# An attention and MoE kernel on one core: ScalarE's copy in the decoding of float64 weights moves 16 bits where it moved 8, and the due times of the order are new

## The chip, the core and the metric

One core of a Trainium2 chip (trn2) runs the whole program. TensorE (PE in the profile) multiplies, ScalarE (ACT), VectorE (DVE) and GpSimd (POOL) do everything else, and SyncE (SP) only issues DMAs. The metric is the device time of one execution in microseconds, the median of several runs.

## The reference

Eight batches of twelve heads of attention over 448 positions with head dimension 64, then a two-layer network with the gate h·cos(h):

```python
def _attn_ref(q, k, v, g_q, g_k):
    q_n, k_n = (rmsnorm(q, g_q), rmsnorm(k, g_k))          # over the last axis
    scores = 1/np.sqrt(64) * np.matmul(q_n, k_n.transpose(0, 1, 3, 2))
    attn = softmax(scores)
    return np.matmul(attn, v).astype(np.float32)           # (8, 12, 448, 64)

def _moe_ref(x, w_in, w_out):                              # x (3584, 768)
    h = x @ w_in                                           # w_in (768, 2048)
    g = h * np.cos(h)
    return (g @ w_out).astype(np.float32)                  # w_out (2048, 768)
```

The two weight matrices come as float64. The kernel reads them as pairs of 32-bit words and makes float32 of them on the chip.

## The kernel before, in words

**Units and phases.** Two heads make a unit `u`; there are 48 units, `NP` = 6 of them to a batch. The first six units are "plain" (float32 matmuls, `score_plain`, `pt_copy`, `av_plain`); all later ones split each operand into a high and a low part (`score`, `pt_high`, `pt_low`, `av`). For each unit PE makes seven score tiles S, DVE scales each by the row's norm and takes its row minimum (`rowmin`, L571), ACT takes the exponential into P (`expo`, L579), PE transposes P into the banks PT0 and PT1 (L613, L618), ACT and DVE copy those to SBUF (L636 and L670 on ACT; L643, L645 and L668 on DVE), and PE multiplies by v (L660, L678). The results of six units are a batch's x; ACT copies them into `xs` (`x_split`, L726) after POOL has scaled them by the row sums (`x_norm`, L717), and then the first layer `ffn1` (L744 to L746) can run on them, 16 blocks of weights `wi` to a batch. The attention of the next batch and `ffn1` of the last one share PE. After the attention comes the second layer (L818 to L820), with PE alone setting the pace.

**The decoding.** Each of 16 blocks of w_in is loaded as 128 x 1536 int32 (`w_load`, `raw` in the profile), and decoded in four steps (`decode`, called by `w_decode`): step 0 on ACT scales the upper words into float32 (L263); step 1 on ACT moves bits of the lower word to the bottom of the upper word (L266); step 2 on DVE shifts the upper word down and keeps its sign and its three lowest bits (L268); step 3 on DVE shifts step 0's result up by three and ORs these bits in (L270). Then ACT rounds the block to its high part (`w_high`, L280) and DVE subtracts that from it (`w_low`, L285). The w_out blocks take the same `decode` with half the width, 32 times (`v_decode`, `rawo` in the profile), between 190 and 861 us.

**What sets the order.** Each engine runs its instructions in the order in which they are written. The class `Plan` writes that order: every piece of work has an engine, a cost, a due time and the keys it reads and writes; a list scheduler takes, on each engine, the ready piece that is due first. The tables `SHIFT`, `PAIR` and `BEGIN` move the due times by kind of work and by unit. `order` uses the costs and due times only while it builds the program; on the chip only the order remains, with semaphores for the dependencies. An instruction whose input is late holds up all that stands behind it on its engine.

Of the kernel before, what the change touches and what calls it, by code (L numbers as in the profile page):

```python
# [13 lines left out]
U8 = mybir.dt.uint8  # L14
# [11 lines left out]
class Plan:  # L26
# [123 lines left out]
    YIELD, AHEAD, WITHIN, UNTIL = ("x_norm", "w_low"), "k_norm", 4.0, 60.0  # L150
# [20 lines left out]
def tile_attention_moe(  # L171
# [14 lines left out]
    NP = NU // B  # L186
    NQT = 7
# [158 lines left out]
    kboth, qlow = {}, [apool.tile([128, 768], F32R, tag="E0", name="E0", bufs=1)]  # L346
# [18 lines left out]
    def e_clear(i):  # L365
        if i:
            qlow.append(apool.tile([128, 768], F32R, tag="E1", name="E1", bufs=1))
# [85 lines left out]
    def rkb(u):  # L453
        return (qtwo[u % 2][:, :S] if u < NP else kboth[u % 2][:, S:]).bitcast(F32)

# [3 lines left out]
    def rk_load(u):  # L459
        if u < NP + 2:  # L460
# [10 lines left out]
    def k_norm(u):  # L471
        if u >= NP:
# [17 lines left out]
    def q_scale(u):  # L490
        q = q_plain(u) if u < NP else qd
        nc.gpsimd.tensor_scalar(q, q, gsc[u < NP], 0.0, op0=ALU.mult, op1=ALU.add)

# [35 lines left out]
    def place(u, n):  # L529
        i = 7 * min(u, NP) + (n if u < NP else 0)  # L530
        if u < NP:
            return ("ph", i // 4) if i % 4 == 3 else ("S", 3 * (i // 4) + i % 4)
        return ("S", i - i // 4 + 7 * (u - NP) + n)

    NSP = 7 * NP // 4
# [72 lines left out]
    def transp(u, kc, part, last):  # L608
        k = KS[kc]
        if kc < 3:  # L610
            for i, t in enumerate(TILES[part]):
                c = k + 64 * (t > 3)
                nc.tensor.transpose(pt[part][:, i * 128 : i * 128 + 128], p_rows(u, t)[:, c : c + 128], ident)  # L613
        else:
            flat = pbuf.rearrange("p n s -> p (n s)")
            for t in range(3):
                e = S * (p_slot(p_key(u, t)) + 1)
                nc.tensor.transpose(pt[0][:, t * 128 : t * 128 + 128], flat[:, e - 64 : e + 64], ident)  # L618
            c, n = (k - 64, 128) if u < NP else (k, 64)
# [215 lines left out]
    def y_store(b, oc, src):  # L835
# [5 lines left out]
        "av": (5.3, 39.33, 0.0), "av3": (-13.83, 15.47, 0.0), "av_plain": (0.0, 0.0, 10.94),  # L841
        "d_place": (7.71, -0.4, 0.0), "e_clear": (2.06, 0.0, 0.0), "e_place": (-13.2, 0.0, 0.0),
        "expo": (7.95, 14.26, -11.58), "ffn1": (-3.18, -2.89, 0.0), "g_fold": (0.0, 0.0, 3.13),
        "g_load": (0.0, 0.0, 0.98), "h_both": (-29.07, 0.0, 0.0), "h_out": (-14.91, 5.31, 0.0),
        "h_store": (-0.09, 0.0, 0.0), "k_high": (7.68, 8.19, 0.0), "k_load": (0.0, 0.0, 1.22),
        "k_low": (33.26, 1.74, 0.0), "k_norm": (45.02, 0.0, -0.54), "kn_copy": (0.0, 0.0, -13.33),
        "kn_load": (0.0, 0.0, -45.16), "kn_norm": (0.0, 0.0, -20.32), "kn_pow": (0.0, 0.0, 29.13),
        "kn_reduce": (0.0, 0.0, -2.77), "kn_square": (0.0, 0.0, -6.31), "kn_turn": (0.0, 0.0, 1.63),
        "kq_load": (-17.42, -14.74, 0.0), "m_place": (-18.39, 4.08, 0.0), "pt_copy0": (0.0, 0.0, -3.9),
        "pt_copy1": (0.0, 0.0, -44.97), "pt_high0": (-25.09, -5.18, 0.0), "pt_high1": (-9.32, -33.28, 0.0),  # L850
        "pt_low0": (-20.85, 10.99, 0.0), "pt_low1": (-5.79, -41.16, 0.0), "q_high": (-79.7, 2.11, 0.0),
        "q_load": (0.0, 0.0, 5.21), "q_low": (-2.0, 3.7, 0.0), "q_scale": (-57.44, -11.45, -3.1),
# [12 lines left out]
    }
    PAIR = (18.33, 10.11, -12.21, 0.63, 7.01, 13.7, -4.94, -21.21, -1.78, 0.0, -39.42, -0.16)
    BEGIN = {"v_load": -5.46, "q_load": 4.31, "v_fetch": -9.59, "st_load": -5.63, "w_load": 12.81, "k_load": 10.48, "kq_load": -37.77, "v_plain": -2.91}

    def add(eng, cost, due, fn, *args, **more):
# [3 lines left out]
        if name in ("ffn1", "h_out", "h_store", "h_both", "x_split"):  # L873
            stage = int(first < (NP if name == "x_split" else 1))
        elif name[:2] not in ("w_", "v_", "e_") or name in ("v_load", "v_high", "v_low", "v_plain", "e_place"):
            stage = 2 if first < NP else int(first < NP + 3)
# [5 lines left out]
        if name in ("w_load", "w_decode", "w_high", "w_low"):  # L882
            due += -0.33 * first
        if name in ("ffn1", "h_out", "h_store", "h_both") and not first:
            due += -0.23 * args[1]
        if name in ("v_fetch", "v_decode", "v_sum", "v_split", "v_store"):
            due += 2.55 + 25.482 * first
# [3 lines left out]
        if more.get("start"):  # L891
            late = BEGIN.get(name0, 0.0) + (0.075 * first if name0 == "w_load" else 0.0)
            more["start"] = max(0.0, more["start"] + late)
# [9 lines left out]
    def base(u):  # L903
        return 14.0 + (PER0 * u if u < NP else PER0 * NP + PER * (u - NP))
# [7 lines left out]
    def weights(fc):  # L912
# [4 lines left out]
        if f64:  # L917
            for step, eng, cost in ((0, ACT, 0.84), (1, ACT, 0.84), (2, DVE, 0.74), (3, DVE, 1.27)):
# [3 lines left out]
        for hf in range(2):  # L922
            add(DVE, 0.53, d, w_low, fc, hf, nc.vector, r=[f, w], w=[("wlo", fc, hf)])
# [40 lines left out]
    def prepare(u):  # L964
# [4 lines left out]
        turned, plain = u < NKT, u < NP  # L969
# [21 lines left out]
        add(SP, ISS, D0 - 45, st_load, u, w=sd, kb=224.0 if turned else 448.0, start=0.0 if u < NP else D0 - 60)  # L991
# [32 lines left out]
    def attend(u):  # L1024
        D0 = base(u)
        b, cc = divmod(u, NP)
        plain = u < NP
        step = 3.0 if plain else 4.0
        lead = 0.0 if u < NP else None
# [127 lines left out]
    for b in range(B):  # L1157
# [5 lines left out]
        if not b:  # L1163
            for i in range(RING["E"]):
                add(DVE, 0.56, 24.0 + 45 * i, e_clear, i, w=[("E0", i)] + [("km", 4)] * i + [("E", NP + i)], start=20.0)
# [188 lines left out]
```

## Time and profile before

| | |
|---|---|
| median of three runs | 1362.52 us (1362.02 to 1363.71) |
| profiled execution | 1365.0 us, of which the program's span is 1363.2 us |
| PE busy | 1339.7 us, 98% of the span, 6998 matmuls |
| DVE busy | 1013.0 us, 74% |
| ACT busy | 977.6 us, 72% |
| POOL busy | 579.1 us, 42% |
| copies of 8 bits on ACT, w_in | 16, 31.7 us in all |
| copies of 8 bits on ACT, w_out | 32, 34.6 us in all |

The span runs from the first instruction to the last one. The busy shares are means over stages that differ: the stretch up to 125 us, where the plain units run and most of w_in is decoded, the stretch up to about 250 us, and the rest.

### The profile page before, as it was taken

To read this page: it belongs to the slowest core of one execution; us is meant where nothing else is said; L and a number is where in the kernel's file an instruction comes from. 1 tells how busy PE (TensorE), PEld (TensorE's weight loads), DVE (VectorE), ACT (ScalarE), POOL (GpSimd) and SP (SyncE) were. 2 spreads that over 40 slices of the span, in tenths; PEclk is the share of its full clock that TensorE was granted. 3 is DMA by queue.
4 is the path that set the end of the run, shared out by engine and by line. 5 is a ranking of instruction groups with operands and counts; after the bars stand their busy time and mean duration, and the time that the engine had idled before them with its cause. 6 is when DMAs were issued, how large, how long until landed. Compare 5 with 4: busy or idle time off the path is not lost.

```text
span 1363.2 us, 21477 instructions
## 1 busy us (share of the span) xinstructions
PE 1339.7 (98%) x6998; PEld 1173.4 (86%) x6998; DVE 1013.0 (74%) x1795; ACT 977.6 (72%) x1920; POOL 579.1 (42%) x522
## 2 busy tenths in 40 slices
PE   6998999999999999999999999999999999999998
PEld 3447888988989899899898889999999999999998
DVE  5988887677777767677767776518889889889743
ACT  7999988787887888787887787646566366366321
POOL 4576657676765866765765675310000000000000
PEclk9998999999999999999999999999999999999999
DMA  6998879889898898898888878248989369369334
GB/s 209 263 286 221 178 192 236 227 240 245 237 234 219 216 245 222 212 256 227 215 221 229 219 208 225 88 176 278 332 287 311 111 246 315 107 246 316 104 113 153
DMA packets 149472, 302.19 MB, mean 222 GB/s; under 512 B 34368, under 2 KB 83088, under 8 KB 149360
## 3 DMA queue, kind: packets, MB, share of 16 engines
q1 hardware_dynamic: 149360, 300.83, 76.8%
q8 instruction: 55, 0.90, 0.3%
q14 instruction: 57, 0.47, 0.1%
HBM read 193.99 MB, written 62.73 MB: 188 GB/s over the span
## 4 chain that ended last, share of the span: by engine, by line
PE 87%; ACT 5%; DVE 3%; POOL 2%; issue 2%; DMA 1%; SPq 0%; ACTq 0%; POOLq 0%; DVEq 0%
PE y L819 10%; PE y L818 10%; PE y L820 10%; PE ph L744 9%; PE ph L745 9%; PE ph L746 9%; PE S L567 8%; PE PT L613 7%; PE O L660 5%; PE O L662 3%; ACT P L579 1%; PE y L746 1%; PE y L744 1%; PE y L745 1%; PE PT L618 1%
## 5 line engine op out<-in xcount | busy, mean ns | idle before, releaser
L571 DVE TENSOR_SCALAR_CACHE_REDUCE S<-S,r 128x448 f32<-128x448 f32 x336 | 224.8, 686 | 59.4 <-PE S L567 49.6
L744 PE MATMUL ph<-xs,wi 128*128 128x448 f32 x660 | 250.7, 380 | 0.2 <-ACT hbuf L762 0.2
L819 PE MATMUL y<-g,wo 128*128 128x448 f32 x672 | 245.4, 365 | 0.0
L818 PE MATMUL y<-g,wo 128*128 128x448 f32 x672 | 245.4, 365 | 0.0
L820 PE MATMUL y<-g,wo 128*128 128x448 f32 x672 | 245.4, 365 | 0.0
L745 PE MATMUL ph<-xs,wi 128*128 128x448 f32 x660 | 242.2, 367 | 0.0
L746 PE MATMUL ph<-xs,wi 128*128 128x448 f32 x660 | 241.4, 366 | 0.0
L579 ACT ACTIVATE P<-S,sm 128x448 f32<-128x448 f32 x336 | 214.4, 644 | 26.2 <-DVE S L571 23.7
L800 ACT CAST g<-gq 128x896 fp32r<-128x896 f32 x112 | 105.7, 943 | 172.8 <-PE y L820 172.3
L636 ACT CAST hi<-PT 128x512 fp32r<-128x512 f32 (+1 forms) x336 | 172.5, 538 | 73.1 <-PE PT L620 42.9
L643 DVE TENSOR_TENSOR lo<-PT,hi 128x512 fp32r<-128x512 f32 x252 | 151.4, 617 | 49.3 <-ACT hi L636 48.7
L798 DVE TENSOR_TENSOR g<-gq,g 128x896 fp32r<-128x896 f32 x112 | 122.0, 1089 | 61.5 <-ACT g L800 61.1
L613 PEld LDWEIGHTS PT<-ident,P 128*128 128x128 f32 x1008 | 120.7, 140 | 37.0 <-ACT hi L670 6.0
L613 PE MATMUL PT<-ident,P 128*128 128x128 f32 x1008 | 146.2, 274 | 1.8 <-DVE lo L643 1.5
L744 PEld LDWEIGHTS ph<-xs,wi 128*128 128x128 f32 x660 | 124.4, 188 | 13.9 <-ACT hbuf L762 1.4
L819 PEld LDWEIGHTS y<-g,wo 128*128 128x128 f32 x672 | 126.2, 188 | 10.0
L820 PEld LDWEIGHTS y<-g,wo 128*128 128x128 f32 x672 | 126.2, 188 | 10.0
L818 PEld LDWEIGHTS y<-g,wo 128*128 128x128 f32 x672 | 126.2, 188 | 10.0
L746 PEld LDWEIGHTS ph<-xs,wi 128*128 128x128 f32 x660 | 124.2, 188 | 10.7
L745 PEld LDWEIGHTS ph<-xs,wi 128*128 128x128 f32 x660 | 124.7, 189 | 8.7
L399 POOL TENSOR_TENSOR r<-r,nhalf 128x14 f32<-128x14 f32 (+1 forms) x48 | 122.6, 2554 | 4.0
L660 PE MATMUL O<-hi,vs 128*128 128x448 f32 x336 | 118.7, 370 | 0.0
(125 smaller groups left out, 2588.4 us busy)
## 6 DMA issues: line engine op xcount, KB each, us to landing
wo<-wo_d SPq DMA_DIRECT2D x152, 384.0 KB
gq<-h_d SPq DMA_DIRECT2D x64, 448.0 KB
h_d<-hbuf SPq DMA_DIRECT2D x54, 448.0 KB
wo_d<-ao SPq DMA_DIRECT2D x56, 384.0 KB
sd<-sd SPq DMA_DIRECT2D x46, 448.0 KB
kq<-kq SPq DMA_DIRECT2D x42, 480.0 KB
D<-qhi SPq DMA_DIRECT2D x84, 192.0 KB
raw<-w_in SPq DMA_DIRECT2D x16, 768.0 KB
```

The lines of the kernel that those rows point to most:

```text
L571: nc.vector.tensor_scalar(d["S", t][:, :S], d["S", t][:, :S], d["r"][:, t : t + 1], None, op0=ALU.mult, op1=ALU.min, accum_out=d["sm"][:, ...
L579: nc.scalar.activation(p_rows(u, t), d.pop(("S", t))[:, :S], AF.Exp, bias=sm[:, 1, t : t + 1], scale=-1.0, accum_out=sm[:, 2, t : t + 1],)
L613: nc.tensor.transpose(pt[part][:, i * 128 : i * 128 + 128], p_rows(u, t)[:, c : c + 128], ident)
L636: nc.scalar.copy(hi if kc < 3 else hi[:64], pt_rows(u, kc, part))
L643: nc.vector.tensor_tensor(lo, src, hi.bitcast(F32), ALU.subtract)
L660: nc.tensor.matmul(O, st, d["hi", kc][:, HEADS[hh]], start=(kc == 0), stop=(kc == 3))
L744: nc.tensor.matmul(ph[:, :S], whi, x2[:, 0, :], start=(cc == 0), stop=False)
L745: nc.tensor.matmul(ph[:, :S], whi, x2[:, 1, :], start=False, stop=False)
L746: nc.tensor.matmul(ph[:, :S], wlo, x2[:, 0, :], start=False, stop=(cc == NCC - 1))
L818: nc.tensor.matmul(y, whi, hi[:, e], start=first and e == 0, stop=False, **more)
L819: nc.tensor.matmul(y, whi, lo[:, e], start=False, stop=False, **more)
L820: nc.tensor.matmul(y, wlo, hi[:, e], start=False, stop=last and e == NG - 1, **more)
```

## The change

In step 1 of `decode` ACT copies, in every 8-byte pair of words, 16-bit number 1 (the upper half of the lower word) over 16-bit number 2 (the lower half of the upper word); before, it copied byte 3 over byte 4. Step 2 then shifts by 13 in place of 5, so that the same three bits arrive in the same place. The number of elements of each of the four steps stays as it was. In the planner, the costs of step 3 on DVE (1.27 to 1.0) and of `w_low` (0.53 to 0.6) are other numbers, that of step 1 stays 0.84, and all the due times are new. `w_low` leaves the list `YIELD`. `NF` = 6 takes the place of `NP` where "plain" is meant (both are 6), and the tile `E0` is made in `e_clear`.

```diff
-            by = st.bitcast(U8).rearrange("p (n t) -> p n t", t=8)
-            nc.scalar.copy(by[:, :, 4], by[:, :, 3])
+            words = st.bitcast(U16).rearrange("p (n t) -> p n t", t=4)
+            nc.scalar.copy(words[:, :, 2], words[:, :, 1])
         elif step == 2:
-            nc.vector.tensor_scalar(up, up, 5, SIGN_LOW, op0=ALU.arith_shift_right, op1=ALU.bitwise_and)
+            nc.vector.tensor_scalar(up, up, 13, SIGN_LOW, op0=ALU.arith_shift_right, op1=ALU.bitwise_and)
...
-    YIELD, AHEAD, WITHIN, UNTIL = ("x_norm", "w_low"), "k_norm", 4.0, 60.0
+    YIELD, AHEAD, WITHIN, UNTIL = ("x_norm",), "k_norm", 4.0, 60.0
...
-        "w_load": (-3.56, 0.0, 0.0), "w_low": (2.76, 0.0, 0.0), "x_half": (-1.22, 1.78, 0.0),
+        "w_low": (8.87, 0.0, 0.0), "x_half": (-15.11, 3.84, 0.0), "x_norm": (-0.93, -13.53, 2.55),
...
-            for step, eng, cost in ((0, ACT, 0.84), (1, ACT, 0.84), (2, DVE, 0.74), (3, DVE, 1.27)):
+            for step, eng, cost in ((0, ACT, 0.84), (1, ACT, 0.84), (2, DVE, 0.74), (3, DVE, 1.0)):
...
-            add(DVE, 0.53, d, w_low, fc, hf, nc.vector, r=[f, w], w=[("wlo", fc, hf)])
+            add(DVE, 0.6, d, w_low, fc, hf, nc.vector, r=[f, w], w=[("wlo", fc, hf)])
```

What the new due times do to the order is small in most places. All engines keep their counts of instructions but for a few; what moves is some places up or down. Lines of the changed kernel are one higher than those of the kernel before (L266 is L267 there). The first number in a name is the unit or the block: `hi5_0` is the copy of unit 5's transposed P, `S7_0` a score tile of unit 7, `raw8` block 8 of w_in, counted from 0.

The first place is on ACT, near 86 us of the profile before, where the plain units end. Before:

```order
L266 COPY raw7_577<-raw7_577 128x768
L579 ACTIVATE P_109,sm5_707<-S5_2_785,sm5_707 128x448
L726 CAST xs_837<-xf0_324 128x448
L726 CAST xs_837<-xf2_596 128x448
L670 COPY hi4_2_847<-PT0_110 128x512
L579 ACTIVATE P_109,sm5_707<-S5_3_812,sm5_707 128x448
L579 ACTIVATE P_109,sm6_827<-S6_3_828,sm6_827 128x448
L495 CAST qhi7_862<-kq_108 128x512
L670 COPY hi5_0_870<-PT0_110 128x512
```

And of the change:

```order
L580 ACTIVATE P_108,sm5_728<-S5_2_786,sm5_728 128x448
L671 COPY hi4_2_838<-PT0_109 128x512
L727 CAST xs_841<-xf0_324 128x448
L727 CAST xs_841<-xf2_613 128x448
L727 CAST xs_841<-xf3_720 128x448
L727 CAST xs_841<-xf1_508 128x448
L580 ACTIVATE P_108,sm5_728<-S5_3_829,sm5_728 128x448
L496 CAST qhi7_864<-kq_107 128x512
L703 COPY xf4_869<-O4_0_761 64x448
L588 ACTIVATE sm5_728<-sm5_728 128x7
L671 COPY hi5_0_881<-PT0_109 128x512
```

`hi4_2` now stands ahead of the copies into `xs`, and the copy of block 7 has gone further up; four copies into `xs` now stand together ahead of `hi5_0`.

The second place is on DVE, from 108 to 117 us of the profile before (`lo6_1` and `lo6_2` free the banks into which PE transposes next). Before:

```order
L268 TENSOR_SCALAR raw8_631<-raw8_631 128x768
L643 TENSOR_TENSOR lo6_1_1055<-PT0_110,hi6_1_1048 128x512
L643 TENSOR_TENSOR lo6_1_1055<-PT1_111,hi6_1_1048 128x384
L592 COPY rt6_1069<-PT1_111 7x128
L270 SCALAR_TENSOR_TENSOR wf8_1003<-wf8_1003,raw8_631 128x768
L571 TENSOR_SCALAR S7_0_1071,sm7_988<-S7_0_1071,r7_681 128x448
L571 TENSOR_SCALAR S7_4_1076,sm7_988<-S7_4_1076,r7_681 128x448
L571 TENSOR_SCALAR S7_5_1082,sm7_988<-S7_5_1082,r7_681 128x448
L285 TENSOR_TENSOR wi8_1102<-wf8_1003,wi8_1102 128x384 x2
L268 TENSOR_SCALAR raw9_673<-raw9_673 128x768
L643 TENSOR_TENSOR lo6_2_1130<-PT0_110,hi6_2_1126 128x512
```

And of the change, from the same `lo6_1` on (the step on block 8 has moved up to stand just ahead of `lo6_0`, and step 3 of that block ahead of these rows):

```order
L644 TENSOR_TENSOR lo6_1_1057<-PT0_109,hi6_1_1046 128x512
L572 TENSOR_SCALAR S7_0_1052,sm7_990<-S7_0_1052,r7_691 128x448
L644 TENSOR_TENSOR lo6_1_1057<-PT1_110,hi6_1_1046 128x384
L593 COPY rt6_1082<-PT1_110 7x128
L572 TENSOR_SCALAR S7_4_1059,sm7_990<-S7_4_1059,r7_691 128x448
L572 TENSOR_SCALAR S7_5_1064,sm7_990<-S7_5_1064,r7_691 128x448
L286 TENSOR_TENSOR wi8_1070<-wf8_960,wi8_1070 128x384 x2
L572 TENSOR_SCALAR S7_1_1103,sm7_990<-S7_1_1103,r7_691 128x448
L394 TENSOR_REDUCE r10_1130<-sd10_1012 128x14
L644 TENSOR_TENSOR lo6_2_1136<-PT0_109,hi6_2_1125 128x512
```

Step 2 of block 9 has gone from just ahead of `lo6_2` to behind it, and one row minimum and one sum of squares have come in its place.

The third place is the start of SP's queue (`kn` are the first unit's keys, `gs` the gains). Before:

```order
L413 DMA kq_108<-kn 112x512
L413 DMA kn1_116<-kn 112x512
L386 DMA sd0_118<-sd 128x448 x2
L228 DMA gs_93<-gg 128x4
L488 DMA q6_99<-kq 128x512 x2
```

And of the change:

```order
L229 DMA gs_93<-gg 128x4
L414 DMA kq_107<-kn 112x512
L387 DMA sd0_116<-sd 128x448
L414 DMA kn1_118<-kn 112x512
L387 DMA sd0_116<-sd 128x448
L489 DMA q6_99<-kq 128x512 x2
```

The load of the gains is now issued first, ahead of the first keys.

## Rows read from the trace of the kernel before

**Rows 1.** Busy us (instructions) of PE, PEld, DVE, ACT, POOL by stretch; clock, DMA share, GB/s.

```profile
20.00:95.00 75.00, 71.66 (x322) 32.01 (x323) 64.80 (x145) 70.37 (x140) 42.95 (x37) 1.00 0.91 275
95.00:125.00 30.00, 26.19 (x122) 18.33 (x121) 26.12 (x52) 27.17 (x58) 23.59 (x21) 0.89 1.07 259
125.00:250.00 125.00, 122.04 (x673) 108.13 (x672) 105.89 (x219) 113.71 (x239) 82.25 (x70) 1.00 0.81 194
250.00:1350.00 1100.00, 1099.61 (x5814) 1001.58 (x5813) 804.68 (x1355) 754.92 (x1459) 419.47 (x380) 1.00 0.76 223
110.00:120.00 10.00, 6.19 (x28) 4.77 (x28) 10.00 (x18) 9.56 (x20) 6.35 (x7) 0.79 1.08 255
120.00:130.00 10.00, 10.00 (x52) 9.04 (x51) 7.87 (x16) 8.06 (x17) 6.49 (x6) 0.87 0.80 174
```

**Rows 2.** Groups of instructions, whole span: busy us, mean ns of one, idle before them.

```profile
L571 DVE TENSOR_SCALAR_CACHE_REDUCE S<-S,r 128x448 f32<-128x448 f32 x336 | 224.8, 686 | 59.4 <-PE S L567 49.6 <-PE S L551 3.5 <-POOL r L398 2.4
L393 DVE TENSOR_REDUCE r<-sd 128x14 f32<-128x896 f32 (+1 forms) x48 | 50.9, 1061 | 4.1 <-ACT sd L390 3.9
L266 ACT COPY rawo<-rawo 128x384 uint8<-128x384 uint8 x32 | 34.6, 1082 | 0.6
L266 ACT COPY raw<-raw 128x768 uint8<-128x768 uint8 x16 | 31.7, 1982 | 0.1
L263 ACT ACTIVATE aq<-rawo 128x384 f32<-128x384 f32 x32 | 17.9, 560 | 1.3 <-POOL ao L328 1.1
L263 ACT ACTIVATE aq<-raw 128x768 f32<-128x768 f32 x8 | 7.6, 947 | 1.2 <-issue 1.2
```

**Rows 3.** Timeline near 69 us: start, us, engine, line; in brackets idle time before, and what ended it.

```profile
67.06 1.96 ACT L266 COPY raw<-raw 128x768 uint8<-128x768 uint8 x1
68.70 0.68 ACT L579 ACTIVATE P<-S,sm 128x448 f32<-128x448 f32 x1
69.52 0.64 PE L551 MATMUL S<-km,q 128*128 128x448 f32 x1 [1.13 <-ACT P L579]
```

**Rows 4.** Timeline near 88 us.

```profile
86.02 2.01 ACT L266 COPY raw<-raw 128x768 uint8<-128x768 uint8 x1
...
88.27 1.13 ACT L726 CAST xs<-xf 128x448 fp32r<-128x448 f32 x2
...
89.20 0.69 ACT L670 COPY hi<-PT 128x512 f32<-128x512 f32 x1
...
89.94 0.59 PE L678 MATMUL O<-hi,vs 128*64 128x448 f32 x1 [0.99 <-ACT hi L670]
```

**Rows 5.** Timeline from 107 to 117 us.

```profile
107.75 0.88 DVE L268 TENSOR_SCALAR raw<-raw 128x768 int32<-128x768 int32 x1 [1.45 <-ACT raw L266]
...
109.37 1.99 ACT L266 COPY raw<-raw 128x768 uint8<-128x768 uint8 x1
...
112.87 0.63 ACT L579 ACTIVATE P<-S,sm 128x448 f32<-128x448 f32 x1
...
113.65 0.47 PE L567 MATMUL S<-M,D 128*128 128x448 f32 x1 [1.08 <-ACT P L579]
...
114.90 1.49 DVE L268 TENSOR_SCALAR raw<-raw 128x768 int32<-128x768 int32 x1
...
116.31 1.14 DVE L643 TENSOR_TENSOR lo<-PT,hi 128x512 fp32r<-128x512 f32 x2
...
117.04 0.69 PE L618 MATMUL PT<-ident,P 128*128 128x128 f32 x2 [2.72 <-DVE lo L643]
```

**Rows 6.** Timeline near 222 us, the copy of a w_out block.

```profile
219.79 1.09 ACT L266 COPY rawo<-rawo 128x384 uint8<-128x384 uint8 x1
...
224.75 0.47 PE L567 MATMUL S<-M,D 128*128 128x448 f32 x1 [1.11 <-ACT P L579]
```

**Rows 7.** Timeline of SP's queue at the start; the second number is the issue.

```profile
2.58 0.43 SPq L228 DMA_DIRECT2D gs<-gg  x1
```

**Rows 8.** Timeline of POOL near 72 us.

```profile
72.41 0.70 POOL L492 TENSOR_SCALAR kq<-kq,gs 128x512 f32<-128x512 f32 x1 [4.99 <-DMA kq<-kq]
```

More of the change, by code (lines that the diff above doesn't have):

```diff
@@ L13 @@
 I32 = mybir.dt.int32
-U8 = mybir.dt.uint8
+U16 = mybir.dt.uint16
 AF = mybir.ActivationFunctionType
@@ L186, in tile_attention_moe @@
     NP = NU // B
+    NF = 6
     NQT = 7
@@ L453, in rkb @@
     def rkb(u):
-        return (qtwo[u % 2][:, :S] if u < NP else kboth[u % 2][:, S:]).bitcast(F32)
+        return (qtwo[u % 2][:, :S] if u < NF else kboth[u % 2][:, S:]).bitcast(F32)
     def rk_spread(u):
@@ L490, in q_scale @@
     def q_scale(u):
-        q = q_plain(u) if u < NP else qd
-        nc.gpsimd.tensor_scalar(q, q, gsc[u < NP], 0.0, op0=ALU.mult, op1=ALU.add)
+        q = q_plain(u) if u < NF else qd
+        nc.gpsimd.tensor_scalar(q, q, gsc[u < NF], 0.0, op0=ALU.mult, op1=ALU.add)
     def q_high(u):
@@ L529, in place @@
     def place(u, n):
-        i = 7 * min(u, NP) + (n if u < NP else 0)
-        if u < NP:
+        i = 7 * min(u, NF) + (n if u < NF else 0)
+        if u < NF:
             return ("ph", i // 4) if i % 4 == 3 else ("S", 3 * (i // 4) + i % 4)
-        return ("S", i - i // 4 + 7 * (u - NP) + n)
-    NSP = 7 * NP // 4
+        return ("S", i - i // 4 + 7 * (u - NF) + n)
+    NSP = 7 * NF // 4
     def score_plain(u, j):
@@ L618, in transp @@
                 nc.tensor.transpose(pt[0][:, t * 128 : t * 128 + 128], flat[:, e - 64 : e + 64], ident)
-            c, n = (k - 64, 128) if u < NP else (k, 64)
+            c, n = (k - 64, 128) if u < NF else (k, 64)
             nc.tensor.transpose(pt[0][:n, 384:512], p_rows(u, 3)[:, c : c + n], ident)
@@ L875, in add @@
         elif name[:2] not in ("w_", "v_", "e_") or name in ("v_load", "v_high", "v_low", "v_plain", "e_place"):
-            stage = 2 if first < NP else int(first < NP + 3)
+            stage = 2 if first < NF else int(first < NF + 3)
         if name in ("pt_low", "pt_high", "pt_copy", "transp"):
@@ L882, in add @@
         if name in ("w_load", "w_decode", "w_high", "w_low"):
-            due += -0.33 * first
+            due += 0.109 * first
         if name in ("ffn1", "h_out", "h_store", "h_both") and not first:
-            due += -0.23 * args[1]
+            due += -0.497 * args[1]
         if name in ("v_fetch", "v_decode", "v_sum", "v_split", "v_store"):
-            due += 2.55 + 25.482 * first
+            due += -1.02 + 25.026 * first
         other = ("w_load", "w_decode", "w_high", "w_low", "v_fetch", "v_decode", "v_sum", "v_split", "v_store", "e_clear")
@@ L891, in add @@
         if more.get("start"):
-            late = BEGIN.get(name0, 0.0) + (0.075 * first if name0 == "w_load" else 0.0)
+            late = BEGIN.get(name0, 0.0) + (0.042 * first if name0 == "w_load" else 0.0)
             more["start"] = max(0.0, more["start"] + late)
@@ L903, in base @@
     def base(u):
-        return 14.0 + (PER0 * u if u < NP else PER0 * NP + PER * (u - NP))
+        return 14.0 + (PER0 * u if u < NF else PER0 * NF + PER * (u - NF))
     def ffn_due(b, i):
@@ L990, in prepare @@
             add(SP, ISS, D0 - 34, kq_load, u, w=kd + qd, kb=480.0, start=D0 - 40)
-        add(SP, ISS, D0 - 45, st_load, u, w=sd, kb=224.0 if turned else 448.0, start=0.0 if u < NP else D0 - 60)
+        add(SP, ISS, D0 - 45, st_load, u, w=sd, kb=224.0 if turned else 448.0, start=0.0 if u < NF else D0 - 60)
         if plain:
@@ L1026, in attend @@
         b, cc = divmod(u, NP)
-        plain = u < NP
+        plain = u < NF
         step = 3.0 if plain else 4.0
-        lead = 0.0 if u < NP else None
+        lead = 0.0 if u < NF else None
         def soften(t, n, key, due):
@@ L1164, in tile_attention_moe @@
             for i in range(RING["E"]):
-                add(DVE, 0.56, 24.0 + 45 * i, e_clear, i, w=[("E0", i)] + [("km", 4)] * i + [("E", NP + i)], start=20.0)
+                add(DVE, 0.56, 24.0 + 45 * i, e_clear, i, w=[("E0", i)] + [("km", 4)] * (i * (NF > 5)) + [("E", NF + i)], start=20.0)
         multiply(b, NFC if b < B - 1 else NEAR)
```

63 lines of the change are left out of this document (31 added, 32 removed).

## The prediction

> **What bounds the kernel now.** I read the busy times by stretch first, because the shares of the whole span hide the stage that matters. From 250 to 1350 us PE is busy for 1099.6 of 1100 us at full clock [rows 1]: whatever ACT, DVE or the order do there, no more than 0.4 us of PE's idle time is to be had. PE's work is the same before and after, so the time can only change where PE stands still or runs at its lower clock, and that is before 250 us: 75.0 - 71.66 = 3.3 us of idle time from 20 to 95 us, 3.8 from 95 to 125, and 3.0 from 125 to 250, together 10.1 us [rows 1]. To that comes the clock: granted 0.79 from 110 to 120 us and 0.87 from 120 to 130, with 1.00 in the long stretches around [rows 1]. In those stretches ACT is the fullest engine behind PE: 70.4 of 75 us, then 27.2 of 30, then 113.7 of 125, with DVE at 64.8, 26.1 and 105.9 [rows 1].
>
> Next I looked up the copy. One of 768 elements takes 1982 ns, one of 384 takes 1082 ns [rows 2], so an element costs (1982 - 1082) / 384 = 2.34 ns. Step 0 reads the same upper words, one in every 8 bytes too, and writes 32 bits: 947 and 560 ns [rows 2], 1.01 ns an element. The slow thing in the decoding is this copy.
>
> Last I went to each place where PE stands still, in the timeline, and asked what it waits for and what stood ahead of that on its engine. At 69.52 us PE has stood for 1.13 us for an exponent, and on ACT this exponent stands right behind a copy of 1.96 us [rows 3]. At 89.94 it has stood for 0.99 us for a copy out of PSUM, which stands behind a copy of 2.01 us and two copies into `xs` [rows 4]. At 113.65 it has waited 1.08 us for an exponent that comes behind the copy at 109.37, and at 117.04 another 2.72 us for a subtraction on DVE; DVE had itself stood for 1.45 us for a copy at 107.75, and step 2 of the next block, 1.49 us, stands right ahead of that subtraction [rows 5]. At 224.75 it waits 1.11 us behind the decoding of a w_out block [rows 6]. These five are 7.0 of the 10.1 us, and each has the copy in its chain.
>
> **The change, part by part.** *The price of the 16-bit copy.* No row shows one. From below, the nearest row is step 0, with the same step in memory and the same number of elements: 0.95 us for a block of w_in and 0.56 for one of w_out [rows 2]. From above it is the present copy, 1.98 and 1.08 us: part of a word is still written, and it may be that which costs. I take the lower end, since step 0 is nearest in everything but the width, and the saving is then 1.98 - 0.95 = 1.04 us for each of 16 and 1.08 - 0.56 = 0.52 us for each of 32. That makes 33 us on ACT, nearly all of it in stretches where PE doesn't wait for ACT; only the chains above count.
>
> The Trainium skill, in ScalarE: Activation LUTs, section What ACT_TABLE_LOAD costs, gives 186 ns plus 0.833 ns for each element, for fp32 and bf16 alike; an estimate by that page is 0.83 us for 768 elements, and the first term below would be 1.1 in place of 1.0. It says nothing of 8 or 16-bit integers.
>
> *At 69.52* the exponent comes 1.04 us sooner: -1.0 us, nearly the whole wait.
>
> *At 89.94* the order helps as well: `hi4_2` now stands ahead of the copies into `xs`, and the copy of block 7 has gone up: the 0.99 us go whole, -1.0 us.
>
> *From 113 to 117* the copy of block 9 has moved behind the exponent that PE awaits, so the 1.08 us go. Ahead of `lo6_2` on DVE three things leave: the wait of 1.45 us, step 2 of block 8 (0.88) and that of block 9 (1.49), 3.82 us [rows 5]. A row minimum and a sum of squares come in their place, 0.69 + 1.06 = 1.75 us [rows 2]. The subtraction is 2.07 us sooner, of a wait of 2.72. Together -3.1 us; bounds 0 (something else is late in the same place) and -3.8.
>
> *The clock* follows that stall: in the 20 us from 110 to 130 us, (0.21 + 0.13) x 10 = 3.4 us of full-speed work are missing [rows 1]. While PE stands still a lower clock costs nothing; if all of the 2.72 us at 117 fell in the spell at half speed, 1.4 of it is no loss. I take 2.0 us, and all of it saved when the stall has shrunk to less than a microsecond: -2.0, bounds 0 and -3.4.
>
> *At 224.75* the shorter copy is worth 0.52 us: -0.5. The 1.5 us of idle time that is left after 125 us I leave as it is.
>
> *What the order costs.* SP now issues the load of the gains first, 0.43 us [rows 7], and the first keys, with which everything begins, come that much later: +0.4 us. And ahead of `hi5_0` on ACT four copies into `xs` stand together, 4 x 1.13 / 2 = 2.26 us [rows 4], where one exponent more, 0.63 [rows 5], stood before: `hi5_0` comes 1.6 us later behind `hi4_2`, and PE needs its bank: +1.6 us, bounds 0 (ACT is ahead by the copies that it saved) and +2.3.
>
> The other numbers of the planner change nothing but the order. DVE's steps 2 and 3 keep their sizes and so their time. The new order after 250 us is hidden under PE, which waits there for nearly nothing; if it opened a wait, there is no cover for it.
>
> *The sum:* -1.0 - 1.0 - 3.1 - 2.0 - 0.5 + 0.4 + 1.6 = -5.6 us. The profiled execution took 1365.0 us for a span of 1363.2, so the next would take 1359.4; the median of the runs lies 2.5 below the profiled one, and the median that I forecast is 1362.5 - 5.6 = 1356.9 us.
>
> **The rivals.** Faster and slower are meant by 0.2%, 2.7 us, which is about what a measurement of this kernel can tell from no change: under 1359.8 and over 1365.2.
>
> *The copy gets no cheaper.* For it: the same 768 or 384 places are written with the same 8 bytes between them, and no row of ACT shows a write with that step at a good rate. Against it: step 0 reads with that step at 1.01 ns [rows 2]. ACT then has as much to do as before and the new order only deals the lateness out anew: I count the 1.0 at 89.94, half of the 3.1 and of the 2.0, and the costs: -1.0 - 1.5 - 1.0 + 0.4 + 1.6 = -1.5, 1361.0 us. Chance 0.14. The Trainium skill, in Advanced Engine Details and Errata, section SBUF Cachelines, states that the rate hangs on hits in 16-byte lines, two of which are wanted on each; the copy touches the same lines before and after, so by that rule its price would not change, and this rival is what would come of it. Step 0's reads agree with the rule's two hits, the 2.34 ns of the present copy, with as many, do not.
>
> *DVE or a DMA is late in ACT's place.* DVE has 26.1 of 30 us filled around the big stall, the DMA engines' share is 1.07 there [rows 1]. Then the 2.72 us and the clock stay: -1.0 - 1.0 - 1.1 - 0.5 + 0.4 + 1.6 = -1.6, 1360.9 us. Chance 0.20.
>
> *Nothing is handed back.* ACT reaches the four copies early enough, and the small waits go too: all of the 10.1 us at best, 1352.5 us. Chance 0.12.
>
> *Slower.* The place is the four copies into `xs`. They read what POOL made, and POOL runs in order: at 72.41 us it had stood for 4.99 us for a load [rows 8]. If that load comes later and the product for `xs` stands behind it, ACT stands in the middle of its queue with `hi5_0` behind it. Price: 5.0 + 1.6 us of PE's time, and after a stall of twice the size twice the 2.0 us for the clock, 10.6 us; without the term at 89.94 and the 1.6 already counted, the rest of the sum is -6.2, so +4.4: 1366.9 us. It decides from a stall of about 3.3 us on. Against it: the product of unit 3 keeps its place in POOL's order, and before the change ACT's copies into `xs` waited for nothing. Chance 0.09.
>
> **How the numbers follow.** The forecast, -5.6 with the bounds of its terms, 1354.5 to 1359.8, has 0.45. With the bigger gain (0.12) and about 0.05 from the better edge of the two middle rivals, faster has 0.62; same has 0.29; slower 0.09. The range from 1352.5 to 1363.0 leaves out the slower rival and some of the tails beyond the bigger gain, together under 0.2.
>
> **What would show it.** In the profile of the changed kernel the copy should stand with 0.9 to 1.0 us for 768 elements and 0.5 to 0.6 for 384; the idle time of PE from 20 to 125 us should fall from 7.1 us to about 3.5; the granted clock from 110 to 130 us should be near 1.00; PE's first wait should end some 0.4 us later; and the stretch from 250 us on should be as full as before. I am wrong if the copy still takes about 2 us, if PE's idle time stays above 9 us before 250 us, or if a stall with a fall of the clock has only moved to another place.

## The result and the profile after

The changed kernel takes 1377.85 us (median of 4 runs, 1377.01 to 1378.2) against 1362.27 us (4 runs, 1361.33 to 1363.71) before: a ratio of 1.0097, 95% interval 1.0082 to 1.0113. It is slower by 15.6 us, on the other side of no change from the forecast of 1356.9 and outside its range. The profiled execution took 1378.2 us, its span 1376.4.

The groups of the copy on ACT, over the whole span of the changed kernel, answer to [rows 2]:

```profile
L267 ACT COPY rawo<-rawo 128x384 uint16<-128x384 uint16 x32 | 34.6, 1081 | 0.7
L267 ACT COPY raw<-raw 128x768 uint16<-128x768 uint16 x16 | 31.5, 1968 | 0.2
```

1968 and 1081 ns, where the 8-bit copy took 1982 and 1082: the price has not moved. The stretches of the changed kernel, in the columns of [rows 1]:

```profile
20.00:95.00 75.00, 72.79 (x318) 31.38 (x318) 64.04 (x147) 71.74 (x143) 41.78 (x36) 1.00 0.91 277
95.00:125.00 30.00, 24.40 (x113) 16.61 (x112) 23.42 (x51) 27.84 (x55) 23.53 (x20) 0.91 1.00 263
125.00:250.00 125.00, 123.08 (x666) 107.83 (x665) 98.49 (x204) 109.08 (x227) 80.97 (x71) 0.99 0.80 189
250.00:1350.00 1100.00, 1099.14 (x5765) 991.89 (x5766) 802.88 (x1359) 754.14 (x1465) 422.21 (x380) 1.00 0.76 221
110.00:120.00 10.00, 6.32 (x34) 4.57 (x32) 8.49 (x20) 9.93 (x17) 8.76 (x7) 0.99 1.06 278
120.00:130.00 10.00, 9.33 (x39) 8.50 (x40) 6.79 (x13) 7.98 (x18) 3.38 (x5) 0.66 0.46 102
```

PE's idle time from 20 to 250 us is 2.2 + 5.6 + 1.9 = 9.7 us, where it was 10.1: it has been dealt out anew, not reduced, and from 20 to 125 us it is 7.8 where the forecast had about 3.5. The waits near 69, 90 and 225 us are gone ([rows 3], [rows 4], [rows 6]), but a stall as long as the big one of [rows 5] stands a little later, and it is an exponent on ACT that ends it, where it was a subtraction on DVE. The timeline of the changed kernel there, with the rows of ACT ahead of it:

```profile
117.03 1.96 ACT L267 COPY raw<-raw 128x768 uint16<-128x768 uint16 x1
118.71 1.16 ACT L637 CAST hi<-PT 64x512 fp32r<-64x512 f32 x2
119.89 0.63 ACT L580 ACTIVATE P<-S,sm 128x448 f32<-128x448 f32 x1
...
120.67 0.74 PE L568 MATMUL S<-khi,qhi 128*128 128x448 f32 x1 [2.94 <-ACT P L580]
```

The exponent stands again behind a copy of 1.96 us. It is the eleventh of the 16 copies of w_in, which before ran ten microseconds later:

```profile
127.26 1.99 ACT L266 COPY raw<-raw 128x768 uint8<-128x768 uint8 x1
```

The granted clock falls behind the stall to 0.66 from 120 to 130 us. From 110 to 130 us (0.01 + 0.34) x 10 = 3.5 us of full-speed work are missing in this execution, 3.4 in that of the kernel before.

The larger part of the loss is in the stretch that I had called full. From 250 to 1350 us PE is busy for 1099.1 of 1100 us at a clock of 1.00, as before, and yet it starts 5765 matmuls where it had started 5814. The same row from 900 to 1300 us, where PE has no waits in either kernel, shows it alone; first before:

```profile
900.00:1300.00 400.00, 400.00 (x1976) 370.65 (x1975) 327.61 (x338) 227.50 (x265) 0.00 (x0) 1.00 0.68 238
```

and then the changed kernel:

```profile
900.00:1300.00 400.00, 400.00 (x1938) 363.26 (x1937) 322.53 (x333) 225.03 (x263) 2.07 (x3) 1.00 0.69 238
```

In both, PE is busy for 400.00 of 400 us at full clock; it is the count that differs, and with it the weight loads' time (PEld in the rows): 370.65 against 363.26 us. In the timeline, the first and the tenth matmul from 1000 us on (here before) are 1.82 us apart,

```profile
999.80 0.36 PE L819 MATMUL y<-g,wo 128*128 128x448 f32 x1
...
1001.62 0.36 PE L819 MATMUL y<-g,wo 128*128 128x448 f32 x1
```

and 1.86 us in the changed kernel:

```profile
999.69 0.37 PE L820 MATMUL y<-g,wo 128*128 128x448 f32 x1
...
1001.55 0.37 PE L820 MATMUL y<-g,wo 128*128 128x448 f32 x1
```

The starts in the trace, in nanoseconds, show two rhythms. Before, distances of 199, 207, 202, 203 and 202 ns follow one another again and again: 202.67 ns in the mean, the **short rhythm**. In the changed kernel there are only 206 and 207: 206.67 ns, the **long rhythm**. Each is steady from the last matmul of the attention (at 887.5 and 891.4 us) to the end. That is some 2325 matmuls, and 2325 x 4.0 ns = 9.3 us of the 15.6; from start to start the last 2325 span 471.0 us before and 480.3 after. These matmuls stand in both programs in the same order and read the same addresses in SBUF; only the PSUM banks of some of them are rotated.

### The profile page after: what moved, and what is told of

It reads as the page before. It is cut to its first block, busy times and chain, and to the rows that moved or that the text cites. A ratio compares the mean times of both kernels' runs of the same rounds, so it can differ in the third digit from the quotient of the medians.

```text
span 1376.4 us, 21467 instructions
## 1 busy us (share of the span) xinstructions
PE 1352.5 (98%) x6998; PEld 1173.8 (85%) x6998; DVE 1006.4 (73%) x1795; ACT 976.9 (71%) x1920; POOL 580.0 (42%) x522
## 4 chain that ended last, share of the span: by engine, by line
PE 87%; ACT 4%; DVE 2%; DMA 2%; POOL 2%; issue 1%; SPq 1%; ACTq 0%; POOLq 0%
PE y L821 10%; PE y L820 10%; PE y L819 10%; PE ph L745 9%; PE ph L746 9%; PE ph L747 9%; PE S L568 8%; PE PT L614 7%; PE O L661 5%; PE O L663 3%; PE y L745 1%; PE y L746 1%; PE y L747 1%; PE PT L619 1%; ACT P L580 1%
## 5 line engine op out<-in xcount | busy, mean ns | idle before, releaser
L637 ACT CAST hi<-PT 128x512 fp32r<-128x512 f32 (+1 forms) x336 | 169.7, 539 | 68.0 <-PE PT L621 47.4
```

Source lines behind the costliest of these rows:

```text
L637: nc.scalar.copy(hi if kc < 3 else hi[:64], pt_rows(u, kc, part))
```

## The experiments

*The order alone.* The changed kernel with the old copy and the old shift:

```diff
-            words = st.bitcast(U16).rearrange("p (n t) -> p n t", t=4)
-            nc.scalar.copy(words[:, :, 2], words[:, :, 1])
+            by = st.bitcast(U8).rearrange("p (n t) -> p n t", t=8)
+            nc.scalar.copy(by[:, :, 4], by[:, :, 3])
...
-            nc.vector.tensor_scalar(up, up, 13, SIGN_LOW, op0=ALU.arith_shift_right, op1=ALU.bitwise_and)
+            nc.vector.tensor_scalar(up, up, 5, SIGN_LOW, op0=ALU.arith_shift_right, op1=ALU.bitwise_and)
```

> The changed kernel with the 8-bit copy and the shift by 5 of before: only the order is new. Theory (the copy costs the same in both widths, 1.97 and 1.08 us, and the order alone makes the difference): 1377.9 us within 1.5, and in the second layer matmuls 206.7 ns apart as in the changed kernel. Rival (the 16-bit copy disturbs something, a neighbour on the memory or DVE's step behind it): back at about 1362 us.

Measured: 1376.54 us against 1364.47 of before, ratio 1.0086 (1.0066 to 1.0107). From 900 to 1300 us PE has 1938 matmuls, as the changed kernel. *The copy alone*, with the same lines exchanged the other way round in the kernel before:

> The kernel before with the 16-bit copy and the shift by 13: only the copy is new, the order is the old one. Theory: copies of 1.97 and 1.08 us, 1362.3 us within 1.5, matmuls of the second layer 202.7 ns apart in the mean, as before. Rival (the copy itself is what costs): above 1370 us.

Measured: 1364.8 us against 1364.47, ratio 1.0002 (0.9993 to 1.0011), copies of 1984 and 1081 ns, 1976 matmuls from 900 to 1300 us. So the order makes the difference (12.1 us alone, with an interval that overlaps that of the whole change), and the width of the copy makes none that can be seen. The rhythm goes with the order in every profile taken: from 910 to 950 us, ahead of any extra matmul, PE starts 199 matmuls in the six programs with the old order and 195 or 196 in the eight with the new one.

*One matmul more at the way into the second layer*, in the changed kernel:

```diff
+    nudged = []
...
+            if not nudged:
+                nudged.append(1)
+                nc.tensor.matmul(banks[bank][:64, :S], whi[:, :64], hi[:, e], start=True, stop=True)
             nc.tensor.matmul(y, whi, hi[:, e], start=first and e == 0, stop=False, **more)
```

> The changed kernel with one matmul more, of 64 weight columns, at the entrance of the second layer (its result is overwritten by the matmul behind it). Addresses, PSUM banks and the order of all else stay. Theory (PE keeps the rhythm with which it enters a stream without waits: 206.7 ns from one matmul to the next in the changed kernel, 1013 ns for five in the kernel before): the extra matmul throws the rhythm over, the distance falls to 199 to 203 ns, and with some 2240 matmuls the time falls by 8 to 9 us, to about 1369. If it falls back into the same rhythm, 1378 and 206.7 ns, which leaves the theory open. Rival (operands, banks or the traffic of other engines set the distance): 206.7 ns and 1378 us.

Measured: 1377.58 us, ratio 1.0089 (1.0074 to 1.0105), and 1937 matmuls from 900 to 1300 us: behind the extra matmul the long rhythm returned within two matmuls. The run left the theory open, so I tried many widths in one kernel:

```diff
+    EXTRA = [16, 32, 48, 64, 96, 128, 160, 192, 224, 256, 288, 320, 352, 384, 400, 416]
...
+            if first and e == 0 and o == 0:
+                cols = EXTRA.pop(0)
+                nc.tensor.matmul(y[:, :cols], whi, hi[:, e, :cols], start=True, stop=True)
```

> The changed kernel with 16 matmuls more in the second layer, one ahead of each of 16 groups (each is overwritten by the matmul behind it), of 16, 32, 48, 64, 96, 128, 160, 192, 224, 256, 288, 320, 352, 384, 400 and 416 columns in this order. Theory (PE keeps the rhythm that the last short matmul left it in): behind some of them the distance changes from 206.7 ns to the 202.7 of the kernel before or another value, and it stays so until the next one; the 16 matmuls cost 3 to 4 us, and each stretch of some 140 matmuls that changes gives 0.6 us back. Rival (operands, PSUM banks or other engines set it, or 206.7 is the only steady rhythm there): 206.7 ns behind every one, 1381 us.

Measured in a single run: 1374.35 us, beside 1365.23 for the kernel before. Behind 9 of the 16 extra matmuls the short rhythm runs, behind 7 the long one, and each holds to the next extra matmul. Three stretches of 40 us, PE alone (busy, instructions, clock, DMA share, GB/s): ahead of the first extra matmul, behind the third (48 columns) and behind the eleventh (288):

```profile
910.00:950.00 40.00, 40.00 (x195) 1.00 0.83 293
987.00:1027.00 40.00, 40.00 (x199) 1.00 0.83 292
1192.00:1232.00 40.00, 40.00 (x195) 1.00 0.61 216
```

195, 199, 195 matmuls in the same time (a matmul that reaches into a stretch counts). No third rhythm appears: all 16 stretches have 206.67 or 202.67 ns. But for the extra matmuls the instructions are those of the changed kernel, operands, addresses and PSUM banks included, and there the long rhythm runs throughout: none of these sets the rhythm alone. *The one of 16 columns alone*:

```diff
+            if n == 0 and first and e == 0 and o == 0:
+                nc.tensor.matmul(y[:, :16], whi, hi[:, e, :16], start=True, stop=True)
```

> The changed kernel with one matmul of 16 columns more, at the entrance of the second layer; nothing else is changed. Two steady rhythms were seen there, 206.67 and 202.67 ns from one matmul to the next in the mean, and 16 columns at this place threw the slow one over into the fast one. Theory: from there on 202.67 ns for some 2016 matmuls, 4.0 ns x 2016 = 8.1 us less, 0.1 us for the extra matmul: 1369.9 us, within 1.5. Rival (the times of the single looks differed for another reason): 1377.9 us.

Measured: 1369.36 us against 1363.61, ratio 1.004 (1.0028 to 1.0053). The expectation of 1369.9 holds. The timeline at the extra matmul, and a stretch of 40 us on either side of it:

```profile
954.01 0.37 PE L747 MATMUL y<-xs,wi 128*128 128x448 f32 x1
954.21 0.17 PE L819 MATMUL y<-g,wo 128*128 128x16 f32 x1
954.24 0.45 PE L821 MATMUL y<-g,wo 128*128 128x448 f32 x1
954.52 0.36 PE L822 MATMUL y<-g,wo 128*128 128x448 f32 x1
954.72 0.36 PE L823 MATMUL y<-g,wo 128*128 128x448 f32 x1
```

```profile
910.00:950.00 40.00, 40.00 (x195) 1.00 0.85 296
960.00:1000.00 40.00, 40.00 (x199) 1.00 0.88 316
```

The changed kernel has 195 from 960 to 1000 us. One extra matmul, which costs 0.1 us, takes 4.0 ns from each of the next 2013, 8.1 us in all. *The other way round*, in the kernel before, first with one matmul of 32 columns:

```diff
+            if n == 0 and first and e == 0 and o == 0:
+                nc.tensor.matmul(y[:, :32], whi, hi[:, e, :32], start=True, stop=True)
```

> The kernel before with one matmul of 32 columns more at the entrance of the second layer; nothing else is changed. 32 columns threw the fast rhythm over into the slow one in the changed kernel. Theory: 206.67 ns from there on, 8.1 us more than before, 1372.6 us; since the fast rhythm has five places at which the extra matmul can fall, it may also stay at 202.67 ns and the time then within 1.5 us of before, 1364.5 on that chip. Rival (the order of the kernel before holds the fast rhythm by itself, through what the other engines do): 202.67 ns.

Measured: 1364.01 us against 1363.61, ratio 1.0002 (0.9991 to 1.0014), 1976 matmuls from 900 to 1300 us: the short rhythm held, which the theory allowed and the rival asked for. Sixteen widths, with the lines that take `cols` from a list, told them apart:

```diff
+    EXTRA = [96, 192, 288, 16, 32, 48, 64, 96, 128, 160, 192, 224, 256, 288, 320, 416]
```

> The kernel before with 16 matmuls more in the second layer, of 96, 192, 288, 16, 32, 48, 64, 96, 128, 160, 192, 224, 256, 288, 320 and 416 columns in this order, each overwritten by the matmul behind it. Theory (two steady rhythms, either of which the kernel can be thrown into): some stretches at 206.67 ns, the others at 202.67, none in between, and the time up by 0.6 us for each slow stretch of 144 matmuls. Rival (the order of the kernel before holds the fast rhythm, as the one extra matmul of 32 columns left it): 202.67 ns behind all 16.

Measured in a single run: 1369.98 us against a median of 1363.55 for the kernel before. The long rhythm runs behind 5 of the 16 (the first two, of 96 and 192 columns, among them) and the short one behind 11. Ahead of the first extra matmul, and behind the eleventh (192 columns):

```profile
910.00:950.00 40.00, 40.00 (x199) 1.00 0.87 296
1190.00:1230.00 40.00, 40.00 (x195) 1.00 0.60 212
```

The rival falls: the kernel before can run in either rhythm too.

*Half the copy.* What would the price that I forecast have been worth? In the changed kernel, with half of the elements left uncopied:

```diff
-            nc.scalar.copy(words[:, :, 2], words[:, :, 1])
+            half = slice(0, words.shape[1] // 2)
+            nc.scalar.copy(words[:, half, 2], words[:, half, 1])
```

> The changed kernel, in which step 1 copies only half of the elements (the low bits of the other half are not restored), so that it takes about 1.08 us for a block of w_in and 0.57 for one of w_out: nearly the price on which my forecast stood. If only that price was wrong: the early stalls go, 5 to 6 us less than the changed kernel, about 1372 us. If the new order gives the time back elsewhere: within 1.5 us of 1377.9. If the lighter ACT also changes the way in which PE enters the second layer, the distance there leaves 206.7 ns and the time falls by up to 9 us more.

Measured: 1370.44 us against 1364.47, ratio 1.0038 (1.0024 to 1.0052), with copies of 1071 and 635 ns and the long rhythm to the end. That is 7.1 us less than the changed kernel with the extra matmul that did nothing (1377.58, measured beside it), more than the 5 to 6 expected. Taken without the 9.3 us of the rhythm it is 6.0 - 9.3 = -3.3 us against before, by subtraction. The stall of the changed kernel is still there, behind copies of half the length:

```profile
115.33 1.07 ACT L268 COPY raw<-raw 128x384 uint16<-128x384 uint16 x1
116.13 1.16 ACT L638 CAST hi<-PT 64x512 fp32r<-64x512 f32 x2
117.32 0.64 ACT L581 ACTIVATE P<-S,sm 128x448 f32<-128x448 f32 x1
...
118.10 0.74 PE L569 MATMUL S<-khi,qhi 128*128 128x448 f32 x1 [2.58 <-ACT P L581]
```

*What sets the copy's price.* Four forms of 384 elements, in turn:

```diff
+                nc.scalar.copy(pairs[:, half:, 1], pairs[:, :half, 0])
...
+                nc.scalar.copy(words[:, half:, 2], row[:, :half])
...
+                nc.scalar.copy(row[:, 4 * half : 5 * half], words[:, :half, 1])
...
+                nc.scalar.copy(row[:, 4 * half : 5 * half], row[:, :half])
```

> The changed kernel, in which step 1 of the 16 blocks of w_in moves 384 elements in one of four forms in turn, so that the low bits of w_in come out wrong: 32-bit words with the step of 8 bytes on both sides; 16-bit numbers read in a row and written with the step; read with the step and written in a row; in a row on both sides. The copy with the step on both sides takes 1.07 us for 384 elements. Theory 1 (the step of the write sets the price): 1.07 us for the first two forms, 0.55 to 0.6 for the last two. Theory 2 (a write of less than a word sets it): 0.55 to 0.6 for the first, 1.07 for the second. Theory 3 (integers go slower than float32, whatever the step): 1.07 for all four. Theory 4 (the read of less than a word with a step sets it): 1.07 for the third only. The time should be that of the kernel with half the copies, 1370 us, within 1.5.

Measured, the four forms in the order of the diff (lines 275, 277, 279, 281):

```profile
L277 ACT COPY raw<-raw 128x384 uint16<-128x384 uint16 x4 | 4.3, 1066 | 0.0
...
L279 ACT COPY raw<-raw 128x384 uint16<-128x384 uint16 x4 | 2.2, 539 | 0.1
L275 ACT COPY raw<-raw 128x384 int32<-128x384 int32 x4 | 2.2, 539 | 0.0
L281 ACT COPY raw<-raw 128x384 uint16<-128x384 uint16 x4 | 2.1, 513 | 0.1
```

Only the form that writes 16-bit numbers with a step of 8 bytes is dear. The step alone costs nothing to speak of (539 ns with whole words), nor does a read of 16 bits with the step (539). Theory 2 holds: it is the write of less than a word, with a step, that costs twice. The time, 1372.05 us in a single run, is 0.6 us above the range that was expected.

*A cheap step 1.* So the word is written whole, in the kernel before:

```diff
+        low = st.rearrange("p (n t) -> p n t", t=2)[:, :, 0]
...
-            nc.scalar.copy(by[:, :, 4], by[:, :, 3])
+            nc.scalar.activation(low, words[:, :, 1], AF.Copy, bias=-0.49994, scale=2.0 ** -13)
...
-            nc.vector.tensor_scalar(up, up, 5, SIGN_LOW, op0=ALU.arith_shift_right, op1=ALU.bitwise_and)
+            nc.vector.scalar_tensor_tensor(up, up, SIGN, low, op0=ALU.bitwise_and, op1=ALU.bitwise_or)
```

> The kernel before, in which step 1 writes whole words: the upper half of the lower word, scaled by 1/8192 and rounded down, goes as an int32 into the lower word, and step 2 on DVE takes the sign of the upper word and ORs that in. If the price hangs on the write of less than a word: 0.92 us for 768 elements and 0.56 for 384, 33 us less on ACT; DVE's step 2 becomes an operation with two inputs, by its step 3 some 1.0 and 0.71 us in place of 0.72 and 0.50, 11 us more. The time then falls by 3 to 7 us as with half the copies in the new order, to about 1359.5 if before takes 1364.5. If DVE is what limits there: within 1.5 us of before. If the conversion makes the write as slow as it was: 1.97 us and 1364.5 or more.

Measured: 1364.05 us against 1363.61, ratio 0.9999 (0.9989 to 1.0008). The prices came near the 0.92 and 1.0 us that were expected (step 1 on ACT, step 2 on DVE, blocks of w_in):

```profile
L270 DVE SCALAR_TENSOR_TENSOR raw<-raw 128x768 int32<-128x768 int32 x16 | 17.2, 1074 | 0.8 <-ACT raw L268 0.7
L268 ACT ACTIVATE raw<-raw 128x768 int32<-128x768 uint16 x16 | 14.7, 919 | 0.0
```

The gain did not. The stretches say where it went (idle time of PE 75.0 - 73.38 = 1.6 us, 3.3 in [rows 1], then 30.0 - 24.51 = 5.5, where it had been 3.8):

```profile
20.00:95.00 75.00, 73.38 (x329) 32.38 (x329) 69.22 (x150) 65.74 (x146) 47.25 (x39) 1.00 0.94 278
95.00:125.00 30.00, 24.51 (x115) 17.59 (x115) 25.42 (x46) 23.76 (x53) 23.46 (x19) 0.89 1.05 254
```

and the timeline names the new wait: ACT, no longer late, stands for POOL, and the delay runs on through the rounding of a block on ACT (L282) and `w_low` on DVE (L287) to the subtraction that PE waits for.

```profile
109.44 0.69 POOL L494 TENSOR_SCALAR kq<-kq,gs 128x512 f32<-128x512 f32 x1
...
110.17 0.62 ACT L497 CAST qhi<-kq 128x512 fp32r<-128x512 f32 x1 [3.02 <-POOL kq L494]
111.28 0.57 ACT L481 CAST khi<-kq 128x448 fp32r<-128x448 f32 x1 [0.49 <-POOL kq L475]
111.76 0.83 ACT L282 CAST wi<-wf 128x768 fp32r<-128x768 f32 x1
...
112.62 2.78 DVE L287 TENSOR_TENSOR wi<-wf,wi 128x384 fp32r<-128x384 f32 x2 [1.36 <-ACT wi L282]
115.32 0.95 DVE L270 SCALAR_TENSOR_TENSOR raw<-raw 128x768 int32<-128x768 int32 x1
116.19 1.14 DVE L645 TENSOR_TENSOR lo<-PT,hi 128x512 fp32r<-128x512 f32 x2
...
116.92 0.90 PE L620 MATMUL PT<-ident,P 128*128 128x128 f32 x3 [2.99 <-DVE lo L645]
```

*The whole word for the first eight blocks alone*:

```diff
+            if word:
+                nc.scalar.activation(low, words[:, :, 1], AF.Copy, bias=-0.49994, scale=2.0 ** -13)
+            else:
+                nc.scalar.copy(words[:, :, 2], words[:, :, 1])
...
-        decode(raw[fc], wfl[fc], step)
+        decode(raw[fc], wfl[fc], step, fc < 8)
```

> The kernel before with the whole-word write for blocks 0 to 7 of w_in alone, which are decoded before 95 us; all later blocks copy 16 bits as in the changed kernel. With the whole-word write everywhere PE's idle time fell by 1.7 us from 20 to 95 us and rose by 1.7 from 95 to 125, where ACT had to wait 3.0 us for POOL. If these two are independent: 1.7 us less than before, 1361.9 if before takes 1363.6. If the sooner work of the first blocks is what brings the later stretch out of step: within 0.7 us of before.

Measured: 1363.98 us (11 runs) against 1363.55, ratio 1.0004 (0.9995 to 1.0013): no gain. PE's idle time in the profiled execution was 1.6 us from 20 to 95 and 3.7 from 95 to 125 us, so the two stretches did come apart as I had hoped, and its span, 1360.3 us, is 2.9 below that of the kernel before, 1363.2; the median shows nothing of it. Of these 2.9 us 1.7 are the clock of two single executions (0.83 and 1.00 in the two stretches from 110 to 130 us, 0.79 and 0.87 in [rows 1]); what became of the rest is open.

*Both causes removed*, the changed kernel with the two lines of the whole word and the extra matmul of 16 columns:

> The changed kernel with the whole-word write of step 1 and the extra matmul of 16 columns. If both causes found so far add up: 1377.9 - 7.1 (as with half the copies) - 8.0 (the rhythm) = 1362.8 us, up to 2 us more for DVE's dearer step 2. If the lighter ACT changes the way into the second layer, the rhythm at the extra matmul can be either: then 1362.8 or 1370.9.

Measured: 1364.71 us against 1363.61, ratio 1.0005 (0.9995 to 1.0014), with 1971 matmuls from 900 to 1300 us as behind the 16 columns alone: 1.9 us over the expectation, which had allowed up to 2 for DVE. No version beat the kernel before.

## Why the prediction was wrong

**The premise that a full stretch can't change failed; this is the larger error.** The prediction said of the time from 250 us on that "no more than 0.4 us of PE's idle time is to be had" and that time can only change where PE stands still or runs at its lower clock. Busy time at full clock isn't the same as pace. The order changed the last steps of the attention, PE came out of them in the other rhythm, and 2325 matmuls took 9.3 us more. A weak hint stood in [rows 1]: the weight loads fill 1001.6 of the 1100 us in which PE is busy for 1099.6, so the busy time leaves something unsaid. The Trainium skill, in Perfetto Trace Analysis, section Identifying the Most-Contended Engine, states that the busy share of matmuls is no good measure of how close a kernel is to its limit and names two others in its place, of which the weight loads' share is one; the rows of 900 to 1300 us agree (400.00 in both, 370.65 against 363.26). But no row of before said which rhythm the new order would fall into.

**The price was taken at the wrong end.** I took 0.95 and 0.56 us, "since step 0 is nearest in everything but the width"; it measured 1.97 and 1.08, the upper bound. The sentence that gave that bound, that part of a word is still written, was the right one: a whole word with the same step costs 539 ns, a part of one 1066. The nearest row should have been chosen by what is written, not by what is read. The Trainium skill, in Advanced Engine Details and Errata, section SBUF Cachelines, has the rate hang on hits in lines of 16 bytes; its forecast of an unchanged price came true, but these runs don't bear the rule out: a whole word and a part of one touch the same lines with the same step, and take 539 and 1066 ns.

**The terms.** Of the five, the waits near 69, 90 and 225 us went, and by the order, since the copies are as long as before. The -3.1 did not come. I had checked what leaves DVE ahead of `lo6_2` and that the copy of block 9 goes behind one exponent, but not what comes onto ACT: the copy of block 10 went up from 127 to 117 us, ahead of an exponent that PE then awaited for 2.94 us, and two smaller waits for exponents, 0.59 and 0.83 us, stand at 113 and 116 us where it was one of 1.08. With half the copy the exponent came 2.6 us sooner, but PE reached it 2.2 us sooner too, so the wait shrank from 2.94 to 2.58 only. The -2.0 for the clock did not come either, and its size was that of one execution. The clock from 110 to 130 us differs between executions of one order; the kernels with one extra matmul, which are the old and the new order untouched until 950 us, have the same there, first the old order,

```profile
110.00:120.00 10.00, 6.25 (x31) 4.72 (x30) 10.00 (x18) 9.78 (x20) 6.43 (x7) 0.90 1.08 254
120.00:130.00 10.00, 10.00 (x53) 8.86 (x53) 8.39 (x18) 8.81 (x18) 7.44 (x7) 0.93 0.85 183
```

then the new one:

```profile
110.00:120.00 10.00, 5.83 (x30) 4.11 (x28) 8.48 (x18) 9.93 (x18) 8.40 (x7) 1.00 1.05 272
120.00:130.00 10.00, 9.77 (x47) 8.85 (x48) 7.21 (x13) 8.69 (x19) 4.83 (x5) 0.83 0.74 180
```

Both miss 1.7 us of full-speed work, half of the 3.4 that the -2.0 was taken from, and the order alone missed none (1.00 in both stretches) behind a stall of 2.97 us. With the gains' load first, PE's first matmul starts 0.3 us later (0.4 forecast). The four copies into `xs` took 1.97 us and PE shows no wait behind them: the +1.6 did not come, nor did the mechanism of the slower rival. Without the rhythm, the changed order with a cheap copy is worth -3.3 us by subtraction (half the copy), against the sum of -5.6 and inside its bounds of -8.0 to -2.7. That this part of the forecast was sound is not shown: the one run with both causes removed is 1.1 us above before, or 0.2 below it without the 1.2 us of the matmuls ahead of the extra one and the 0.1 for itself, though with a dearer step 2 on DVE.

**The rivals.** "The copy gets no cheaper" named the right mechanism with 0.14, and its 1361.0 was still far off, as it counted no loss but the two small costs. Without the 9.3 us the new order costs 6.3 us by the result, 2.8 by the order alone, 3.8 by the first extra matmul and, with 1.2 us for the matmuls ahead of it and 0.1 for itself, 4.4 by that of 16 columns. I can place part of it: at the 1150th matmul (250 us) the four profiled executions stand 2.3, 0.0, 2.5 and 0.7 us behind the one before, and between there and the 4650th (some 880 us) each loses a further 1.1 to 1.8 us. The first part is mixed with the clock, which from 110 to 130 us misses 3.5, 0.0, 1.7 and 1.7 us in the four and 3.4 in that of the kernel before. The two kernels with one extra matmul, whose clocks agree up to there, stand 2.7 us apart at that matmul; how much of that is the order and how much the scatter of executions is open. The second part falls in a stretch that is full by busy time, which fits the mix of the two rhythms there but was not tested. "DVE or a DMA late in ACT's place" is near what the cheap step 1 then showed, with POOL as the late one, after 1.3 us of its own for a load.

**What stays open:** what in PE or its weight loads makes the two rhythms, and which step of the order decides between them. That the order decides is shown (order alone and copy alone), and that the instructions of the long stream do not (the extra matmuls). I did not try to restore the last matmuls of the attention to their old places alone.

## What to carry to other kernels

Where PE is the bound, compare matmuls started in equal stretches, or the weight loads' busy time, before arguing about waits: a stretch can lose 2% with no idle time and at full clock. When a change of order loses time far from the place that it touched, look at the rhythm first; an extra matmul of a few columns ahead of the stream is a cheap test, and can be the cure, though which width does it could here only be found by trying. And when an order is new, follow what comes onto an engine ahead of a wait, not only what leaves it. Price an unseen operation by the row that shares its write: a part of a word with a step cost ACT twice the whole word with the same step.

## What the runs showed of the hardware

A stream of matmuls of 448 columns with a weight load for each ran in one of two steady rhythms, 202.67 ns (five in 1013 ns) or 206.67 ns, at a granted clock of 1.00 in both. One matmul of 16 to 416 columns in between could change one into the other or leave it, and it held for up to 400 us, to the end of the stream. On ACT 384 elements took 539 ns with 32-bit words in a step of 8 bytes, 539 when 16 bits are read so and written in a row, 1066 when they are written so, and 8 bits no less (1082). The granted clock from 110 to 130 us was 0.83, 0.91 and 1.00 in three executions of the new order, behind stalls of 2.94, 2.95 and 2.97 us.
